# Chunk 0's diagonal by `v` and the identity in an attention-and-MLP kernel, with fewer idle products and late weights in halves

## The chip, the core and the metric

The kernel runs on one core of a Trainium2 chip. The metric is the device time of one execution in microseconds. In the texts the engines are called PE (TensorE, the matrix engine), DVE (VectorE), ACT (ScalarE), POOL (GpSimd) and SP (SyncE, which here only issues DMAs). "q" counts the four pairs of heads in a chunk of tokens.

## The reference

First a linear attention with a decay `w` and a bonus `u` for the present token, then a two-layer MLP with a leaky activation.

```python
B, H, S, D = 4, 8, 768, 48                       # r, k, v
for t in range(S):
    cur = np.einsum('bhd,bhe->bhde', u[None] * kt, vt)
    y[:, :, t] = np.einsum('bhd,bhde->bhe', rt, state + cur)
    state = w[None, :, :, None] * state + np.einsum('bhd,bhe->bhde', kt, vt)
...
x = y.transpose(0, 2, 1, 3).reshape(B * S, H * D)          # 3072 x 384
h = x @ w_in                                               # 384 x 2048
g = np.maximum(h, 0.0) + alpha * np.minimum(h, 0.0)
return (g @ w_out)                                         # 2048 x 384
```

## The kernel before

The 768 positions are cut into six chunks of 128. In chunk 0 (`first_chunk(q)`, once for each pair q of heads) the attention needs no state. DVE scales `r` and `k` by powers of the decay (L431) and multiplies them elementwise into `prod` (L500). PE sums `prod` with `u` (`c_sum`, L507), which gives the diagonal of the score matrix, `cu`: one number for each position, head and batch, in eight columns of a bank. PE makes the scores of all pairs of positions (`scores`, L442). ACT copies the sums (L511) and writes eight blocks "identity times `cu`" into two `base` tiles (L449); DVE copies the scores of earlier positions over them by a mask (`copy_predicated`, L453); PE multiplies `base` by `v` (`out`, L463). The output is split in a high and a low part, `xh` and `xl` (L389, L392 on ACT, L378, L379 for the last pair), of which pieces are moved to other partitions by small DMAs (`lower`, L367). PE also turns `k` (`turn`, L295), ACT copies it (`kk`, L299), PE makes the chunk's state (L489), and ACT copies that to `T` (L494).

Then come the hidden tiles: 16 tiles of 128 hidden units for each chunk. For one tile and one chunk `m_in` makes nine products of 512 columns (L678: high by high, high by low and low by high, for three slices of the input), ACT and DVE make the activation's high part `gh` and low part `gl` (L686 to L691), and `m_out` adds nine products (L712) into three banks. The order of the tiles is chunk 0 tiles 0 to 8, chunk 1 tiles 0 to 8, chunk 0 and then chunk 1 tiles 9 to 15, then the chunks 2 to 5. The attention of later chunks (`prepare` and `burst`, L533 to L650) is placed between them. The weights of a tile arrive as one load of 768 KB (`wraw`, L323, two buffers) and are put together in `weights`: ACT L343, DVE L345, L347, L350, ACT L353 (`wh`), DVE L354 (`wl`).

A function `warm` (L233) adds a bf16 product of the identity whose result nobody reads, an idle product. It writes the columns 128 to 511 of the bank that also holds chunk 0's diagonal sums. 23 of them stand at the program's start, and `with_warm(n, ...)` puts n ahead of a group of products.

The Python code does not set the engines' order itself. Each `add` hands a planner an engine, an estimated time, the tiles read and written, and a rank; `Plan.in_order` then chooses, for all engines together, what stands next. A new estimate or rank therefore moves other work too.

## Time and profile before

| | |
|---|---|
| median of three runs | 486.32 us (486.3 to 486.8) |
| profiled execution | 486.93 us |
| its span in the trace | 485.2 us |
| around the span | 1.73 us |
| PE busy | 476.6 us, 98% of the span, 4644 records |
| DVE busy | 310.8 us, 64% |
| ACT busy | 247.2 us, 51% |
| POOL busy | 43.5 us, 9% |
| granted clock of PE, mean | 0.995 |

The span begins with the first instruction that the profiler recorded and ends with the last; the execution's own time is a little longer. All starts in the rows below count from the span's start. A row's length runs to the end of the result, so rows of pipelined products overlap; what a group costs its engine is the distance from its start to the next group's.

### The profile page before, as it was taken

To read this page: it belongs to the slowest core of one execution; us is meant where nothing else is said; L and a number is where in the kernel's file an instruction comes from. 1 tells how busy PE (TensorE), PEld (TensorE's weight loads), DVE (VectorE), ACT (ScalarE), POOL (GpSimd) and SP (SyncE) were. 2 spreads that over 40 slices of the span, in tenths; PEclk is the share of its full clock that TensorE was granted. 3 is DMA by queue.
4 is the path that set the end of the run, shared out by engine and by line. 5 is a ranking of instruction groups with operands and counts; after the bars stand their busy time and mean duration, and the time that the engine had idled before them with its cause. 6 is when DMAs were issued, how large, how long until landed. Compare 5 with 4: busy or idle time off the path is not lost.

```text
span 485.2 us, 11237 instructions
## 1 busy us (share of the span) xinstructions
PE 476.6 (98%) x4644; PEld 387.5 (80%) x4644; DVE 310.8 (64%) x518; ACT 247.2 (51%) x578; POOL 43.5 (9%) x49
## 2 busy tenths in 40 slices
PE   8999999999999999999999999999999999999994
PEld 5778878888888888888888888888888878888883
DVE  7789999999786785855755655745644534333331
ACT  5889866776555552553553643444642333433222
POOL 2000010012211011101202202202000000000000
PEclk9999999999999999999999999999999999999998
DMA  8675776642243641431121341121210000100002
GB/s 238 193 209 187 225 242 190 228 157 66 72 131 106 187 136 57 136 103 36 58 83 37 118 119 37 54 75 33 95 26 1 1 1 0 67 0 0 1 1 70
DMA packets 23752, 45.82 MB, mean 94 GB/s; under 512 B 3856, under 2 KB 11408, under 8 KB 23696
## 3 DMA queue, kind: packets, MB, share of 16 engines
q1 hardware_dynamic: 23552, 44.92, 29.6%
q8 instruction: 38, 0.62, 0.6%
q14 instruction: 18, 0.15, 0.1%
q10 hardware_dynamic: 144, 0.13, 0.1%
HBM read 36.38 MB, written 6.29 MB: 88 GB/s over the span
## 4 chain that ended last, share of the span: by engine, by line
PE 88%; DVE 7%; ACT 2%; DMA 1%; issue 1%; POOL 0%; ACTq 0%; DVEq 0%; POOLq 0%
PE acc L712 40%; PE bank L678 38%; PE bank L612 2%; PE acc L233 2%; PE bank L622 2%; PE bank L591 2%; PE bank L584 1%; DVE wl L354 1%; DMA wraw<-wall 1%; DVE wx L350 1%; DVE wx L347 1%; DVE g L687 1%; DVE wx L345 1%; DVE gl L691 1%; ACT wx L343 1%
## 5 line engine op out<-in xcount | busy, mean ns | idle before, releaser
L687 DVE SCALAR_TENSOR_TENSOR g<-bank,alph,g 128x512 f32<-128x512 f32 x96 | 71.9, 748 | 107.0 <-ACT g L686 106.3
L686 ACT ACTIVATE g<-bank 128x512 f32<-128x512 f32 x96 | 57.3, 597 | 137.0 <-PE bank L678 136.5
L678 PE MATMUL bank<-xh,wh 128*128 128x512 f32 x288 | 113.0, 392 | 0.0
L678 PE MATMUL bank<-xh,wl 128*128 128x512 f32 x288 | 112.2, 390 | 0.1
L678 PE MATMUL bank<-xl,wh 128*128 128x512 f32 x288 | 112.1, 389 | 0.0
L691 DVE TENSOR_TENSOR gl<-g,gh 128x512 fp32r<-128x512 f32 x96 | 69.5, 724 | 41.6 <-ACT gh L690 41.4
L690 ACT ACTIVATE gh<-g 128x512 fp32r<-128x512 f32 x96 | 60.5, 630 | 66.1 <-DVE g L687 65.9
L712 PE MATMUL acc<-gh,wh 128*128 128x512 f32 x288 | 83.6, 396 | 0.0
L712 PE MATMUL acc<-gh,wl 128*128 128x512 f32 x288 | 82.0, 391 | 0.0
L712 PE MATMUL acc<-gl,wh 128*128 128x512 f32 x288 | 81.7, 390 | 0.0
L678 PEld LDWEIGHTS bank<-xh,wh 128*128 128x128 f32 x288 | 54.0, 188 | 11.6 <-ACT kk L299 0.3
L678 PEld LDWEIGHTS bank<-xh,wl 128*128 128x128 f32 x288 | 54.1, 188 | 11.5 <-DVE wl L354 0.5
L678 PEld LDWEIGHTS bank<-xl,wh 128*128 128x128 f32 x288 | 54.1, 188 | 11.3
L712 PEld LDWEIGHTS acc<-gl,wh 128*128 128x128 f32 x288 | 54.0, 188 | 11.3
L712 PEld LDWEIGHTS acc<-gh,wl 128*128 128x128 f32 x288 | 53.8, 188 | 11.4
L712 PEld LDWEIGHTS acc<-gh,wh 128*128 128x128 f32 x288 | 52.7, 188 | 11.2
L547 POOL TENSOR_TENSOR rr<-rr,kk 128x384 f32<-128x384 f32 x16 | 22.5, 1405 | 286.2 <-DMA kk<-vkr 227.1
L558 ACT ACTIVATE base<-ident,cu 128x64 f32<-128x64 f32 x160 | 41.5, 337 | 1.0 <-DVE cu L553 0.9
L379 DVE TENSOR_TENSOR xl<-bank,xh 48x256 fp32r<-48x256 f32 (+1 forms) x66 | 28.4, 430 | 1.5
L533 DVE TENSOR_TENSOR raw<-raw,W 112x512 f32<-112x512 f32 x40 | 26.7, 682 | 0.8 <-DMA raw<-rk 0.8
L378 ACT ACTIVATE xh<-bank 48x256 fp32r<-48x256 f32 (+1 forms) x66 | 25.5, 386 | 2.5 <-PE bank L622 1.0
L643 DVE COPY_PREDICATED base<-strict,bank 128x256 f32<-128x256 uint8 x40 | 17.3, 442 | 4.4 <-PE bank L591 4.4
(102 smaller groups left out, 388.2 us busy)
## 6 DMA issues: line engine op xcount, KB each, us to landing
wraw<-wall SPq DMA_DIRECT2D x16, 768.0 KB, 4.7
raw<-rk SPq DMA_DIRECT2D x46, 224.0 KB, 3.9
v<-vkr SPq DMA_DIRECT2D x24, 192.0 KB, 3.6
rr<-vkr SPq DMA_DIRECT2D x16, 192.0 KB, 2.5
kk<-vkr SPq DMA_DIRECT2D x16, 192.0 KB, 3.4
oT<-o SPq DMA_DIRECT2D x12, 256.0 KB, 2.2
oT<-g SPq DMA_DIRECT2D x5, 256.0 KB, 2.8
xh<-xh SPq DMA_DIRECT2D x36, 32.0 KB, 2.0
```

What stands on the lines that cost most here:

```text
L378: add("ACT", us, lambda: nc.scalar.activation(to(h), view(), AF.Copy), r=[src], w=refs(h), rank=rank)
L379: add("DVE", us + 0.1, lambda: nc.vector.tensor_tensor(out=to(l), in0=view(), in1=to(h), op=ALU.subtract), r=[src] + refs(h), w=refs(l), r ...
L533: add("DVE", 0.72, lambda t=t, tab=tab: nc.vector.tensor_tensor(out=t().rearrange("p b (j t) -> p (b j) t", t=span), in0=t().rearrange("p ...
L547: add("POOL", 1.2, lambda: nc.gpsimd.tensor_tensor(out=rt(), in0=rt(), in1=k(), op=ALU.mult), r=[k] + ([wh[12]] if c == 2 else []), w=[rt] ...
L558: add("ACT", 0.32, lambda g=g, b=b: nc.scalar.activation(base()[:, g, b], ident2(), AF.Copy, scale=cu()[:, g, b:b + 1]), r=[cu, ident2], w ...
L643: add("DVE", 0.42, lambda g=g: nc.vector.copy_predicated(base()[:, g], strict2()[:, None, :].broadcast_to([128, B, HI]), A[g]()[:, 0:256]. ...
L678: nc.tensor.matmul(hp()[:, :], a[i]()[:, k], x[c]()[:, k], start=(k == 0 and j == 0), stop=(k == NK - 1 and j == 2))
L686: add("ACT", 0.6, lambda: nc.scalar.activation(g(), hp()[:, :], AF.Copy), r=[hp], w=[g], rank=n - 100)
L687: add("DVE", 0.75, lambda: nc.vector.scalar_tensor_tensor(out=g(), in0=hp()[:, :], scalar=alph()[:, i:i + 1], in1=g(), op0=ALU.mult, op1=A ...
L690: add("ACT", 0.64, lambda: nc.scalar.activation(gh(), g(), AF.Copy), r=[g], w=[gh], rank=n - 100)
L691: add("DVE", 0.73, lambda: nc.vector.tensor_tensor(out=gl(), in0=g(), in1=gh(), op=ALU.subtract), r=[g, gh], w=[gl], rank=n - 99)
L712: nc.tensor.matmul(banks[k](), a[i]()[:, NK + k], x(), start=(begin and j == 0), stop=(end and j == 2))
```

## The change

For chunk 0 the diagonal no longer goes into the score matrix. DVE multiplies `v` by the sums into a tile `vc`, straight from the bank (L475 of the changed kernel), and `out` adds four products of `vc` with the identity for each pair (L495). The `base` tiles get zeros once (`zeroed`, L441) in place of the scaled identity, and the copies `cu` of chunk 0 are gone. Two POOL memsets clear the two tiles that `vc` uses (L375). The number of idle products falls, from two to one or from two or one to none, and the block at the start has five of 512 columns, one for each bank, and 16 of 384 in place of 23 of 384. Raw weights from tile 10 on come in two loads, and tile 2's load is put behind chunk 0's `lower` DMAs.

```diff
     def warm(into):
...
+        idle(into()[:, 128:512])
+
+    def idle(into):
+        x, n = ident().bitcast(mybir.dt.bfloat16), into.shape[1] // 2
+        nc.tensor.matmul(into.rearrange("p (a f) -> p a f", a=2), x[:, 0:128],
+                         x[:, None, 0:n].broadcast_to([128, 2, n]), start=True, stop=True, skip_group_check=True)
...
+        if i < NF - 6:
+            return load(t, lambda: nc.sync.dma_start(t().rearrange("p f a -> p (f a)"), wall[i].bitcast(U32)), 768, rank,
+                        behind)
+
+        for j in range(2):
+            load((t, j), lambda j=j: nc.sync.dma_start(
+                t()[:, DM * j:DM * (j + 1)].rearrange("p f a -> p (f a)"),
+                wall[i].bitcast(U32)[:, 2 * DM * j:2 * DM * (j + 1)]), 384, rank)
...
+            if i == 2:
+
+                for t, at in first_lower:
+                    p.after.update(o for o, part, wr in plan.log[t] if wr and part == at and o.eng == "SP")
...
+    spread = [sb([128, B, 2 * HI], "gh", 3, F32R, mv) for _ in range(2)]
+    for t in spread:
+        add("POOL", 0.6, lambda t=t: nc.gpsimd.memset(t().bitcast(F32), 0.0), w=[t], rank=-70)
...
+    def zeroed(n):
+        if n not in bases:
+            bases[n] = [sb([128, B, L], "gl", 3, F32, mv) if n else sb([128, B, L], "base", 3) for _ in range(2)]
+            for t in bases[n]:
+                add("ACT", 0.6, lambda t=t: nc.scalar.activation(
+                    t(), ident()[:, None, :].broadcast_to([128, B, L]), AF.Copy, scale=0.0), r=[ident], w=[t], rank=-93 + n)
+        return bases[n]
...
-        with_warm(2, 1.05, scores, r=[r, k0], w=A, rank=q - 90).after.add(first)
-        base = [sb([128, B, L], "gl", 3, F32, mv) if q % 2 else sb([128, B, L], "base", 3) for _ in range(2)]
-        for g in range(2):
-            for b in range(B):
-                add("ACT", 0.39, lambda g=g, b=b: nc.scalar.activation(
-                    base[g]()[:, b], ident(), AF.Copy, scale=cu()[:, g, b:b + 1]), r=[cu, ident], w=[(base[g], b)],
-                    rank=-60 + q)
+        with_warm(1, 1.05, scores, r=[r, k0], w=A, rank=q - 90).after.add(first)
+        base = zeroed(q % 2)
+        vc = spread[q % 2]
+        add("DVE", 0.55, lambda: nc.vector.tensor_tensor(
+            out=vc().bitcast(F32).rearrange("p b (g e) -> p g b e", g=2)[:, :, :, 0:D],
+            in0=v().rearrange("p (g b) e -> p g b e", g=2), op=ALU.mult,
+            in1=bank()[:, 8 * q:8 * q + 8].rearrange("p (b g) -> p g b", g=2)[:, :, :, None].broadcast_to([128, 2, B, D])),
+            r=[v, (bank, q)], w=[vc], rank=10 * q - 77)
...
-                        stop=b == B - 1, skip_group_check=True)
-
-        last_out[:] = [with_warm(2, 0.95, out, r=[v] + base, w=[y], rank=q - 85)]
+                        stop=False, skip_group_check=True)
+            for b in range(B):
+                nc.tensor.matmul(y()[0:112, b * L:(b + 1) * L], vc().bitcast(F32)[:, b, 0:112], ident(), start=False,
+                                 stop=b == B - 1, skip_group_check=True)
+
+        last_out[:] = [with_warm(0, 1.45, out, r=[v, vc, ident] + base, w=[y], rank=q - 85)]
...
-            with_warm(1, 0.5, lambda: turn(t, k0), r=[k0, ident], w=[t], rank=-84 + q)
+            with_warm(0, 0.5, lambda: turn(t, k0), r=[k0, ident], w=[t], rank=-84 + q)
...
-            with_warm(1, 0.75, product, r=[k, v], w=[U], rank=-45 + q)
+            with_warm(0, 0.75, product, r=[k, v], w=[U], rank=-45 + q)
...
-        first = with_warm(2 if mine != sums else 0, 0.56, c_sum, r=[prod, uw], w=[mine], rank=sum_rank)
...
+        first = with_warm(1 if mine != sums else 0, 0.56, c_sum, r=[prod, uw], w=[mine], rank=sum_rank)
...
-    add("PE", 6.7, lambda: [warm(bank) for _ in range(23)], r=[ident], w=[(bank, "warm")], rank=-1000)
+
+    add("PE", 6.7, lambda: [idle(t) for t in plan.banks] + [warm(bank) for _ in range(16)], r=[ident], w=[(bank, "warm")], rank=-1000)
```

How the planner's order moves is shown at three places. The first is PE at the diagonal sums and the scores of chunk 0's second pair; `acc_135` (before) and `acc_140` (after) are the bank with the sums and the idle products' results, and a bracket names the engine or DMA queue that a row waits for. Before:

```order
L233 MATMUL acc_135<-ident 128x384 [waits Activation_49]
L233 LDWEIGHTS ident
L233 MATMUL acc_135<-ident 128x384
L507 MATMUL acc_135<-uw,g 64x2 [waits DVE_49]
L507 MATMUL acc_135<-uw,g 64x2 x7
L233 LDWEIGHTS ident
L233 MATMUL acc_135<-ident 128x384
L233 LDWEIGHTS ident
L233 MATMUL acc_135<-ident 128x384
```

After:

```order
L236 MATMUL acc_140<-ident 128x384
L538 MATMUL acc_140<-uw,g 64x2 [waits DVE_49]
L538 MATMUL acc_140<-uw,g 64x2 x7
L236 LDWEIGHTS ident
L236 MATMUL acc_140<-ident 128x384 [waits DVE_49]
```

One idle product has left each pair, and the wait for ACT, which copied the sums out of the bank, has become a wait for DVE at the second idle product.

The second place is DVE from the scaling of the third pair's `k` on. Before (`base` and `gl` are the tiles that the mask writes, `g` is `prod`):

```order
L431 TENSOR_TENSOR raw<-raw,W_78 112x512 [waits DMAHW6_49]
L431 TENSOR_TENSOR o<-o,W_79 112x512 [waits DMAHW7_49]
L453 COPY_PREDICATED base<-strict,bank_117 128x512 [waits PE_49,Activation_49]
L500 TENSOR_TENSOR g<-raw 112x512 [waits DVE_49]
L453 COPY_PREDICATED base<-strict,bank_118 128x512 [waits PE_49,Activation_49]
```

After (`gh` is `vc`):

```order
L459 TENSOR_TENSOR raw<-raw,W_78 112x512 [waits DMAHW6_49]
L475 TENSOR_TENSOR gh<-v,acc_140 128x2x4x48 [waits DMAHW1_49,PE_49]
L481 COPY_PREDICATED base<-strict,bank_117 128x512 [waits Activation_49]
L481 COPY_PREDICATED base<-strict,bank_118 128x512 [waits Activation_49]
L531 TENSOR_TENSOR g<-raw 112x512 [waits DVE_49]
L475 TENSOR_TENSOR gh<-v,acc_140 128x2x4x48 [waits DMAHW2_49,PE_49]
```

The product `vc`, which waits for the load of `v`, now stands right behind the third pair's scaling and ahead of both masks of the first pair; the fourth pair's scalings have moved behind.

The third place is SP, the queue that issues the DMAs, around the end of chunk 0. Before:

```order
L367 DMA xh<-xh_394 16x512 x4
L323 DMA wraw<-wall 128x1536
L367 DMA xh<-xh_394 16x512
L404 DMA raw<-rk 112x512
L367 DMA xh<-xh_394 16x512
L367 DMA xl<-xl_469 16x512 x6
L406 DMA v<-vkr 128x384 x2
```

After:

```order
L383 DMA xh<-xh_318 16x512 x4
L421 DMA raw<-rk 112x512 x3
L383 DMA xh<-xh_318 16x512
L383 DMA xl<-xl_432 16x512 x4
L383 DMA xh<-xh_318 16x512
L383 DMA xl<-xl_432 16x512 x2
L423 DMA v<-vkr 128x384 x4
L577 DMA rr<-vkr 128x384
L327 DMA wraw<-wall 128x1536 x2
```

Tile 2's load `wraw` has moved from among the parts of `xh` to behind all parts, four loads of `v` and one of `rr`.

In the same way the second tile's low weights `wl` now stand on DVE ahead of the first steps of the third tile, chunk 1's sums of one pair stand on PE ahead of the second tile's products, and the third tile's nine products stand behind the next burst of chunk 1, with which also the first `m_out` products have moved ahead of it.

## Rows read from the trace of the kernel before

**Rows 1.** The waits of PE: what it waited for, total us, times, longest.

```profile
PE bank L507 <- DVE g L500: 0.4, 1, 0.4
```

**Rows 2.** PE's timeline: start, length (us), engine, line, operation, tiles, number of instructions.

```profile
1.48 6.58 PE L233 MATMUL acc<-ident 128*128 128x384 bf16 x25 [1.48 <-POOL ident L257]
7.99 0.63 PE L507 MATMUL acc<-uw,g 112*64 112x2 f32 x16
...
11.51 0.50 PE L233 MATMUL acc<-ident 128*128 128x384 bf16 x2
11.93 1.16 PE L442 MATMUL acc<-raw 48*128 48x128 f32 x16
...
21.94 1.09 PE L463 MATMUL bank<-base,v 128*64 128x128 f32 x16
22.96 0.34 PE L233 MATMUL acc<-ident 128*128 128x384 bf16 x1
23.13 0.55 PE L295 MATMUL bank<-ident,raw 112*128 112x112 f32 x4
...
29.38 0.34 PE L233 MATMUL acc<-ident 128*128 128x384 bf16 x1
29.64 0.67 PE L489 MATMUL bank<-v,kk 128*64 128x48 f32 x16
30.26 0.60 PE L295 MATMUL bank<-ident,raw 112*128 112x112 f32 x4
...
30.92 0.50 PE L678 MATMUL bank<-xh,wh 128*128 128x512 f32 x1
...
35.01 0.39 PE L678 MATMUL bank<-xh,wl 128*128 128x512 f32 x1
...
43.01 1.13 PE L612 MATMUL bank<-raw,T 48*48 48x64 f32 x32
...
45.84 0.60 PE L295 MATMUL bank<-ident,raw 112*128 112x112 f32 x4
```

**Rows 3.** Tile `v`, 4 to 14 us: its loads (duration ns), and their time to landing.

```profile
L406 SPq DMA_DIRECT2D v<-vkr x4: 327/378/430, 5.0 to 7.1; - x4
...
DMA to landing us min/median/max: 6.2/6.6/6.8
```

**Rows 4.** DVE's line L411 over the whole run: duration ns min/median/max, first and last start.

```profile
L411 DVE TENSOR_TENSOR kk<-kk,whalf x16: 541/546/1371, 101.8 to 332.5; 128x384 f32<-128x384 f32 x16
```

**Rows 5.** ACT's timeline, 24 to 27 us.

```profile
24.37 0.87 ACT L353 ACTIVATE wh<-wx 128x768 fp32r<-128x768 f32 x1
...
25.53 1.61 ACT L392 ACTIVATE xl<-bank 112x512 fp32r<-112x512 f32 x3
```

**Rows 6.** DVE by lines, 4 to 32 us (busy, mean ns, idle before).

```profile
L453 DVE COPY_PREDICATED gl<-strict,acc 128x512 f32<-128x512 uint8 x4 | 2.9, 737 | 0.6 <-ACT gl L449 0.6
L453 DVE COPY_PREDICATED base<-strict,bank 128x512 f32<-128x512 uint8 x4 | 2.9, 727 | 1.9 <-ACT base L449 1.9
...
L345 DVE TENSOR_SCALAR wx<-wx 128x768 uint32<-128x768 uint32 x3 | 1.7, 561 | 1.4 <-ACT wx L343 1.4
```

**Rows 7.** DVE's timeline: a scaling of chunk 0, and tile 1's last step.

```profile
9.82 0.68 DVE L431 TENSOR_TENSOR raw<-raw,W 112x512 f32<-112x512 f32 x1
...
33.60 0.95 DVE L354 TENSOR_TENSOR wl<-wx,wh 128x768 fp32r<-128x768 f32 x1
```

**Rows 8.** SP's timeline: the issues of DMAs.

```profile
26.56 3.78 SPq L367 DMA_DIRECT2D xl<-xl  x6
```

**Rows 9.** Tile `wraw`, 0 to 70 us: its loads' time to landing.

```profile
DMA to landing us min/median/max: 4.5/6.1/8.8
```

**Rows 10.** Windows around the end: us, busy of PE, PEld, DVE, ACT, POOL, granted clock, DMA.

```profile
470.00:478.70 8.70, 8.70 (x39) 6.91 (x37) 2.15 (x4) 3.06 (x5) 0.00 (x0) 1.00 0.06 24
478.70:480.70 2.00, 0.03 (x1) 0.00 (x0) 0.42 (x1) 0.38 (x1) 0.00 (x0) 1.00 0.74 258
480.70:485.00 4.30, 0.00 (x0) 0.00 (x0) 0.00 (x0) 0.00 (x0) 0.00 (x0) 0.50 0.09 28
```

More of the change, by code (lines that the diff above doesn't have):

```diff
@@ L231, in warm @@
     def warm(into):
-        x = ident().bitcast(mybir.dt.bfloat16)
-        nc.tensor.matmul(into()[:, 128:512].rearrange("p (a f) -> p a f", a=2), x[:, 0:128],
-                         x[:, None, 0:192].broadcast_to([128, 2, 192]), start=True, stop=True, skip_group_check=True)
+        idle(into()[:, 128:512])
[3 more added lines that the diff above has]
+                         x[:, None, 0:n].broadcast_to([128, 2, n]), start=True, stop=True, skip_group_check=True)
     def with_warm(n, us, fn, r, w, rank):
@@ L317, in half_table @@
             pt()[:, :].rearrange("p (m g e) -> p m g e", m=P, g=2)[:, :, :, 0:D], AF.Copy), r=[pt], w=[whalf], rank=-62)
-    raws = {}
+    raws, first_lower = {}, []
     def raw_weights(i, rank, behind=()):
         t = raws[i] = sb([128, 2 * DM, 2], "wraw", 2, U32)
-        p = load(t, lambda: nc.sync.dma_start(t().rearrange("p f a -> p (f a)"), wall[i].bitcast(U32)), 768, rank, behind)
-        return p
+        if i < NF - 6:
[5 more added lines that the diff above has]
+                wall[i].bitcast(U32)[:, 2 * DM * j:2 * DM * (j + 1)]), 384, rank)
     def weights(i, need):
         if i not in raws:
-            raw_weights(i, need - 9)
+            p = raw_weights(i, need - 9)
+            if i == 2:
+                for t, at in first_lower:
+                    p.after.update(o for o, part, wr in plan.log[t] if wr and part == at and o.eng == "SP")
         raw = raws[i]
@@ L367, in dma @@
                     nc.sync.dma_start(t()[to, k].bitcast(F32), y()[HI * g + 16 * k:HI * g + 16 * (k + 1)].bitcast(F32))
+                first_lower.append((t, (k, g)))
                 add("SP", 0.45, dma, r=[top[name]], w=[(t, (k, g))], rank=-40 if c == 0 else -8, kb=32)
@@ L415, in u_rows @@
         return t()[0:112, at:at + B * D].rearrange("p (b e) -> p b e", b=B)
+    bases = {}
+    def zeroed(n):
[5 more added lines that the diff above has]
+        return bases[n]
     def first_chunk(q):
@@ L433, in first_chunk @@
                 r=[W[q]], w=[t], rank=10 * q + j - 90)
-        cu = sb([128, 2, B], "cu", 2)
-        first = diagonal(q, r, k0, cu, bank, slice(8 * q, 8 * q + 8), (bank, q), 10 * q - 88, -95 + q, -70 + q)
+        first = diagonal(q, r, k0, None, bank, slice(8 * q, 8 * q + 8), (bank, q), 10 * q - 88, -95 + q, -70 + q)
         A = [psum() if q % 2 == 0 else pb([128, NT], f"acc{g}") for g in range(2)]
@@ L508, in c_sum @@
                                      stop=True, skip_group_check=True)
-        first = with_warm(2 if mine != sums else 0, 0.56, c_sum, r=[prod, uw], w=[mine], rank=sum_rank)
-        add("ACT", 0.2, lambda: nc.scalar.activation(
-            cu(), sums()[:, cols].rearrange("p (b g) -> p g b", g=2), AF.Copy), r=[mine], w=[cu], rank=copy_rank)
+        first = with_warm(1 if mine != sums else 0, 0.56, c_sum, r=[prod, uw], w=[mine], rank=sum_rank)
+        if cu:
+            add("ACT", 0.2, lambda: nc.scalar.activation(
+                cu(), sums()[:, cols].rearrange("p (b g) -> p g b", g=2), AF.Copy), r=[mine], w=[cu], rank=copy_rank)
         return first
```

## The prediction

> **What bounds the kernel now.** I read the waits of TensorE (PE) first, then its timeline, then the views of those engines that feed it. After its start PE waits at one place for .4 us and at another for less [rows 1]: from 1.48 on it has work without a gap, so the time is the sum of what stands in PE's queue. A saving has to shorten that queue, and it lasts only as long as the data come earlier too. The prelude of chunk 0 ends where the first hidden tile starts, at 30.92 [rows 2]; that place is the measure of most of this change. DVE is the engine with the least room behind it. While it prepared chunk 0 it lay idle .6 + 1.9 + 1.4 = 3.9 us, waiting for ACT's base tiles and for ACT's first step of the weights [rows 6].
>
> **The parts, one by one.** All times are of the profiled execution, 486.93 us (its span of 485.2 and 1.73 around it), which lies .6 above the median of 486.32; the sum is a difference, and I take it off the median.
>
> *Opening block.* 25 idle products take 1.48 to 7.99 [rows 2]. The new block has 22, with 9088 columns in place of 9600: 512 fewer, 1.3 products of 384 at the .17 that one takes later (22.96 to 23.13) [rows 2]: -.2 us.
>
> *The wait for `v`.* This is the one new wait on PE that I can price. DVE's new product `vc` reads pair 0's diagonal sums in the bank in which the idle products write, and the order shows that the second idle product of pair 1 waits for DVE. PE stood there at 11.51; without the block's .2 and two halves of a pair (.42 the pair, 11.51 to 11.93 [rows 2]) it comes at about 10.9. But `vc` needs pair 0's `v`. The first of the four `v` loads is issued at 5.0, and they take 6.2 to 6.8 us [rows 3]; so it lands between 11.2 and 11.8, and I take 11.8, since the loads of all four pairs stand ahead of it. `vc` itself does not occur before. Its nearest row is a product of the same 128x384 shape on DVE, median 546 ns [rows 4]; one operand now lies in a bank, and the bounds are .5 and the .74 of a DVE operation of 512 columns on a bank [rows 6]. It ends at 11.8 + .55 = 12.35, and PE goes on at 12.4: a wait of 1.5 us (bounds .8 and 1.7). Counted against before, PE is .9 late at this place.
>
> *Idle products behind that place.* Between 11.51 and the last turn before the hidden tiles, 30.26, PE spends 18.75 us [rows 2]. In it lie nine pairs at .42 = 3.8, four single products at .17 (as 22.96 to 23.13) and four at .26 (29.38 to 29.64) = 1.7 [rows 2], together 5.5. Five single ones stay, at half a pair, .21: 1.05. So -4.45. Whether the group ahead of a removed idle product also gets shorter no row shows cleanly; it can only add to the gain, and I leave it out.
>
> *Identity products.* Eight f32 products of 128 columns take 21.94 to 22.96, .1275 each [rows 2]. Sixteen more: +2.05 (bounds 1.7, at a seventh less when nothing follows of another kind, and 2.2).
>
> *Check's product*, a short one between the turn at 30.26 and 30.92 [rows 2], leaves the prelude and comes back later: about -.1 here, 0 in all.
>
> The start of the hidden tiles follows: 30.92 + .9 - 4.45 + 2.05 - .1 = 29.3, a gain of 1.6 us.
>
> *Does ACT keep up?* ACT loses 32 `base` activations and four copies and gets four zeroings early, of which each step takes about .5 (as three of 112x512 take 1.61 [rows 5]): 2.0 us while it waits for the tables and for PE's first sums; without that cover PE's turn of the half table would come that much later. The last turn before the tiles waits for ACT's `T`. PE gives pair 2's output at 12.4 + the 11.45 from 11.51 to 22.96 less 3.6 of idle products, + 1.5 for twelve identity products, + 1.05 = 22.8. From there ACT has `xh`, two pairs of `kk`, two `xl`, `wh` (.87), `xh`, `xl`, a pair of `kk`, `xh` and `T`; with a pair of `kk` and each of the others at the half us of an `xl` that is ten halves and .87 [rows 5], 5.9 us: 28.7. PE wants it at 30.26 - 1.6 = 28.7. So ACT is just in time and I set its cost at nothing; bounds 0 and .5.
>
> *Does DVE keep up?* The low part of tile 1's weights is made by 33.60 + .95 = 34.55, and PE first uses it at 35.01 [rows 2, 7]. In the new order PE wants it at 35.01 - 1.6 and, because the sums of one pair now stand ahead of tile 1, .6 later: 34.0. Ahead of it on DVE there is more: four `vc` (2.0) and one more scaling (.6); and less: two steps of tile 2's weights (.56 and .95 [rows 6, 7]) and four tiny operations of the check (.4), 1.9. Idle time falls from 3.9 to the 1.3 for `v` (the scaling that stands ahead of `vc` as it stood before ends at 9.82 + .68 = 10.5 [rows 7]) and something up to .7 while `vc` and the masks follow PE. The net is +2.6 - 1.9 - 3.9 + 2.0 = -1.2: ready at 33.4, in time by .6. Tile 2's products have moved behind a burst (43.01 to 45.84 [rows 2]) and behind 16 products of 512 columns (.223 each, 8.70 us for 39 [rows 10]), so its weights are wanted at about 43.
>
> *Weight loads.* Halves from tile 10 on: PE waits for no weights there before, and six more DMA issues of under .5 us lie on an idle queue; 0 in the sum, and without that cover still under .5 for one tile. Tile 2's load, now behind chunk 0's lower parts, is rival three. Two memsets on POOL lie on an engine with nothing else due then: 0.
>
> Sum: -1.6 us, nearly all of it in the first 30 us, and no part of the stretch from 70 us on changes. 486.93 - 1.6 = 485.3 for the profiled execution, **484.7** against the median. With the bounds (wait .8 to 1.7, identity 1.7 to 2.2, shorter neighbours up to .5, ACT up to .5) the case itself spans 483.9 to 485.5.
>
> **A rule to weigh against this.** At the end of the program the granted clock is still 1.00 for 2.0 us after the last product, and .50 after that [rows 10]; that is the upper of the two levels, 2.4 GHz, then the lower, 1.2. PE's new wait is 1.5 us, shorter than that, so by the row the clock stays and the sum holds. The Trainium skill, "TensorE: Matmul & The Clock Gate", section "HAM oscillation — how this bites in real kernels", says that pauses of PE between groups of products send the clock back to half and that the products after the pause then run cold; by it, with fewer idle products left, the wait would cost a second start at the low level.
>
> **Rival one: the clock falls after the wait for `v` (chance .20).** For: the idle products are what PE did when it had nothing else, and 23 of them go. Against: the wait is shorter than the 2.0 us above, and PE has real products on both sides. The price of a low start can be read off the opening block: 25 products take 6.5 us where 25 at .17 would take 4.25, so 2.3 [rows 2]. -1.6 + 2.3 = +.7: 487.0, and 486.0 if half of the price lies under waits that are there anyway: no change that can be told.
>
> **Rival two: DVE gives the gain back (chance .17).** The margin of .6 at tile 1 rests on DVE's idle time falling by 1.9. Once 1.3 us or more remain beside the wait for `v` (the new `vc` stands in one queue with the masks, and behind it wait the masks, PE's outputs and ACT's `xh`), each further us is a wait of PE at the first tiles. If the idle time stays as it was, DVE is 1.9 late, PE loses 1.3, and the gain is .3: 486.0, the range of this case 485.4 to 486.4.
>
> **Rival three, slower: tile 2's raw weights come late (chance .13).** Before, the load stood between the lower parts; the six `xl` parts end at 26.56 + 3.8 = 30.3 [rows 8]. Now it stands behind all of them, four `v` and one `rr`. The parts come about 2 us earlier, then five issues of about .5 (an issue alone is .33 to .43 [rows 3]): issued at 30.8. Loads of this tile land after 4.5 to 8.8 us, median 6.1 [rows 9]: 36.9, at worst 39.6. From the landing ACT needs .9 and DVE, in the new order, eight operations up to `wl`, four of tile 2's (.56 and three of .95), four others of some 2.5, less .08 of overlap each: 5.3. So 43.1 against the 43 at which PE wants it. Every us of landing later than 37 is a us of PE, and DVE's later tiles shift with it. At 39.6 the loss is 2.5, +.9 in all: 487.2; with one more us, 488.2. For: the margin is none at the median. Against: half of the loads shown land sooner, and this one has few others beside it.
>
> **How the numbers follow.** The forecast has .50: 484.7. The rivals have .20, .17 and .13. What a measurement of this kernel can tell from no change is about 0.2%, 1 us: below 485.35 is faster, above 487.29 slower. Faster: .50 and a little of rival two, .52. Slower: most of rival three and the end of rival one, .12. Same: .36. The range of 8 in 10 goes from the lower bound of the forecast's own case, 483.9, to the 487.2 at which rival three starts to show.
>
> **What would show it.** In the changed profile PE's idle product of pair 1 waits for DVE at about 11, for 1.5 us, and DVE idles there for the `v` load. The first hidden tile starts near 29.3. PE has no wait above .5 between there and 70, and the clock reads 1.00 from 7 to 478. If the hidden tiles start at 29.3 and the end comes as before, look for a wait of PE between 33 and 60 for `wl` (rivals two and three). If the products after 12.4 are spaced twice as far, it is rival one. The prediction is wrong if the wait for `v` is longer than 1.7 us or if PE waits for ACT in the prelude by more than .5.

## The result, and the profile after

The changed kernel takes 490.57 us (median of 16 runs, 487.33 to 492.99); the kernel before, run beside it, takes 486.81 (16 runs, 485.52 to 487.93). The ratio is 1.0075, interval 1.0058 to 1.0091: slower by 3.8 us, where a gain of 1.6 was forecast. The 16 times go with the mean granted clock of PE, which was measured for each execution: 487.33 us at .996, 492.99 at .987, and 14 of the 16 below .995, where the executions of before beside the experiments lie between .995 and .999. By an estimate from the medians of the clock (.991 against .998, over 490 us) some 3.4 of the 3.8 us are time lost at a low clock. The profiled execution took 492.12 us with a span of 490.4, 5.2 longer than before's. "Before" below is the kernel before, "after" the changed one, and "the start" is the first product of the first hidden tile, 30.92 us in before [rows 2].

After's waits of PE, in the form of [rows 1]:

```profile
PE bank L654 <- ACT seen_y L669: 1.8, 1, 1.8
PE bank L236 <- POOL ident L260: 1.5, 1, 1.5
PE bank L616 <- ACT kk L302: 0.8, 1, 0.8
PE acc L236 <- DVE gh L475: 0.7, 1, 0.7
PE bank L710 <- DVE wl L367: 0.5, 1, 0.5
PE bank L298 <- ACT T L525: 0.4, 1, 0.4
```

The 1.5 at the program's start is in before too [rows 2]. The others are 4.2 us where before had .6 (.4 [rows 1], and .2 for `xh` at 67). Their places stand in PE's timeline, in the form of [rows 2]:

```profile
8.23 0.63 PE L538 MATMUL acc<-uw,g 112*64 112x2 f32 x16
...
10.85 0.63 PE L538 MATMUL acc<-uw,g 112*64 112x2 f32 x16
12.19 0.32 PE L236 MATMUL acc<-ident 128*128 128x384 bf16 x1 [0.71 <-DVE gh L475]
12.44 1.16 PE L469 MATMUL acc<-raw 48*128 48x128 f32 x16
...
14.07 1.09 PE L491 MATMUL bank<-base,v 128*64 128x128 f32 x16
15.09 1.13 PE L495 MATMUL bank<-ident,gh 128*112 128x128 f32 x8
16.05 0.33 PE L236 MATMUL acc<-ident 128*128 128x384 bf16 x1
...
30.84 0.60 PE L298 MATMUL bank<-ident,raw 112*128 112x112 f32 x4 [0.38 <-ACT T L525]
31.21 0.47 PE L710 MATMUL bank<-xh,wh 128*128 128x512 f32 x1
...
34.74 0.63 PE L616 MATMUL bank<-v,kk 64*64 64x48 f32 x31 [0.82 <-ACT kk L302]
...
44.02 0.69 PE L654 MATMUL bank<-base,v 64*48 64x64 f32 x16 [1.79 <-ACT seen_y L669]
44.64 0.96 PE L538 MATMUL bank<-uw,g 112*64 112x2 f32 x16
45.53 1.65 PE L744 MATMUL acc<-gh,wl 128*128 128x512 f32 x3
...
48.68 1.48 PE L744 MATMUL acc<-gh,wh 128*128 128x512 f32 x3
```

Three things are to be seen. The start is at 31.21, not at 29.3. The four identity products of a pair (an f32 product shows as two records, so x8) take 15.09 to 16.05, .24 each, beside .13 for each of the eight ahead of them (14.07 to 15.09). And from 45 on three products of 512 columns take twice the usual time: 48.68 to 49.96, 1.28, where three at the .223 of [rows 10] take .67. The windows say why (columns as in [rows 10]):

```profile
13.00:15.00 2.00, 2.00 (x32) 1.65 (x28) 2.00 (x5) 0.55 (x2) 0.00 (x0) 1.00 1.03 320
...
45.00:46.00 1.00, 1.00 (x13) 0.98 (x12) 1.00 (x3) 0.97 (x2) 0.00 (x0) 0.50 0.03 10
...
50.00:51.00 1.00, 1.00 (x4) 0.81 (x3) 1.00 (x4) 0.87 (x2) 0.00 (x0) 0.50 0.91 151
...
52.00:53.00 1.00, 1.00 (x6) 0.81 (x5) 0.43 (x1) 0.00 (x0) 0.00 (x0) 1.00 0.97 401
```

The granted clock is at its upper level (2.4 GHz) after the wait of .71 for `vc`, and at its lower (1.2 GHz) for 6 us after the wait of 1.79. What was late there is a load. SP's timeline, then ACT's:

```profile
34.54 0.86 SPq L327 DMA_DIRECT2D wraw<-wall  x2
```

```profile
41.93 0.89 ACT L356 ACTIVATE wx<-wraw 128x768 f32<-128x768 f32 x1 [2.37 <-DMA wraw<-wall]
42.73 0.54 ACT L302 ACTIVATE kk<-bank 128x192 f32<-128x192 f32 x2
43.15 0.63 ACT L722 ACTIVATE gh<-g 128x512 fp32r<-128x512 f32 x1
43.80 0.17 ACT L669 ACTIVATE seen_y<-bank 1x2 f32<-1x2 f32 x1
```

Tile 2's raw weights are issued at 34.54, behind all parts of chunk 0, and land 7.4 us later. ACT stands 2.37 us in its queue for them, and behind that step waits `seen_y`, which PE needs.

The price of the low clock is read against a run that passes the same place at the upper level, `e5_own_bank` (below):

```profile
43.88 0.96 PE L744 MATMUL acc<-gh,wl 128*128 128x512 f32 x3
...
47.25 0.39 PE L710 MATMUL bank<-xh,wh 128*128 128x512 f32 x1
```

The account of this execution against before: the start +.3; later waits of 1.8, .8 and .5 where before had .4 and .2, +2.5; the low clock +2.8 (45.53 to 51.24 is 5.7 for what takes 3.4 in e5, with .3 more in the `c_sum` ahead and .2 in the product behind). That is 5.6 against the 5.2 of the spans. The products of tiles 2 to 4 stand in another order in the two kernels, and I leave the .4 open.

### The profile page after: what moved, and what is told of

It is laid out like the page before. It is cut to its first block, busy times and chain, and to the rows that moved or that the text cites. A ratio compares the mean times of both kernels' runs of the same rounds, so it can differ in the third digit from the quotient of the medians.

```text
span 490.4 us, 11223 instructions
## 1 busy us (share of the span) xinstructions
PE 478.5 (98%) x4650; PEld 391.7 (80%) x4650; DVE 312.0 (64%) x522; ACT 239.2 (49%) x546; POOL 45.2 (9%) x51
## 4 chain that ended last, share of the span: by engine, by line
PE 89%; DMA 4%; DVE 3%; ACT 2%; SPq 1%; issue 0%; ACTq 0%; DVEq 0%
PE acc L744 40%; PE bank L710 38%; DMA wraw<-wall 3%; PE bank L644 2%; PE bank L654 2%; PE bank L623 2%; PE bank L616 1%; DMA v<-vkr 1%; PE bank L495 1%; PE bank L491 1%; SPq L421 1%; DVE wx L363 1%; ACT wx L356 1%; PE acc L469 0%; DVE wl L367 0%
## 5 line engine op out<-in xcount | busy, mean ns | idle before, releaser
L744 PE MATMUL acc<-gh,wl 128*128 128x512 f32 x288 | 83.4, 396 | 0.0
L654 PE MATMUL bank<-base,v 64*48 64x64 f32 x640 | 19.1, 216 | 1.8 <-ACT seen_y L669 1.8
```

The source lines that it names most:

```text
L654: nc.tensor.matmul(where(g, b, j), v0()[s, g * B + b], base0()[s, g, b], start=False, stop=(crossed == 1 and e == 0), skip_group_check=True)
L744: nc.tensor.matmul(banks[k](), a[i]()[:, NK + k], x(), start=(begin and j == 0), stop=(end and j == 2))
```

## The experiments

All were timed in five rounds, each beside before on its own chip. Medians of runs taken at different times stand beside different runs of before, so the ratio is the surer figure. Each run gives its median, its ratio to before with the 95% interval, and what its own profiled execution shows.

**What an identity product costs.** `e3_ident_halves`, after with every identity product as two of half the width:

```diff
-                nc.tensor.matmul(y()[0:112, b * L:(b + 1) * L], vc().bitcast(F32)[:, b, 0:112], ident(), start=False,
-                                 stop=b == B - 1, skip_group_check=True)
+                for rows in (slice(0, HI), slice(HI, 112)):
+                    nc.tensor.matmul(y()[rows, b * L:(b + 1) * L], vc().bitcast(F32)[:, b, rows], ident(), start=False,
+                                     stop=b == B - 1, skip_group_check=True)
```

> The changed kernel with each identity product split into two, of 64 and of 48 of the 112 columns of vc, which go to the two column halves of PE as out's own products do; 32 products in place of 16, all else in the same order. Theory B (a product over the full width costs .24, and two over half the width each run side by side): the four products of a pair take .96 us in the changed kernel and about .5 here, so the prelude gets 1.9 us shorter up to the wait for ACT's T, and the hidden tiles start at 29.5 to 30.3 in place of 31.2. The end follows only in part, since tile 2's load stays late: 488.5 to 490.5. Rival (the price is by the number of products): the group takes 1.9 us, the hidden tiles start near 35, 492 to 495.

489.26 us, 1.0080 (1.0051 to 1.0109). PE's timeline at the second pair's output, where the clock is at its upper level again:

```profile
20.71 1.04 PE L496 MATMUL bank<-ident,gh 128*48 128x128 f32 x16
21.69 0.34 PE L236 MATMUL acc<-ident 128*128 128x384 bf16 x1
```

Eight halves take .98, as four whole ones took .96: .12 for a half, .24 for a whole. The price goes with the width, and the prediction's .1275 was that of a half.

`e5_own_bank` is told below. On it rest `e9_no_ident`, without the identity products:

```diff
-            for b in range(B):
-                nc.tensor.matmul(y()[0:112, b * L:(b + 1) * L], vc().bitcast(F32)[:, b, 0:112], ident(), start=False,
-                                 stop=b == B - 1, skip_group_check=True)
```

> e5 (the idle product ahead of the scores in its own bank) without the sixteen identity products, so that chunk 0's outputs lack the diagonal's share; DVE still makes vc. It measures what the identity products cost. In the profiles four of them take .96 us, 3.8 in all. If all of it lies on PE's path, the hidden tiles start at 26.7 in place of 30.5 and PE's wait for T grows by nothing. If ACT or DVE then set the pace of the prelude, the start moves by less than 3.8 and the difference shows as waits of PE for masks, T or wl: start 27.5 to 29.5, time 485 to 487. If tile 2's load and chunk 1's v loads stay where they are, the end moves less than the start.

and `e10_turned`, in which PE writes `vc` turned (a transposition against the identity) and adds `out`'s products onto it:

```diff
+                nc.tensor.matmul(y()[0:112, b * L:(b + 1) * L], vc().bitcast(F32)[:, b, 0:112], ident(), start=b == 0,
+                                 stop=False, is_transpose=True, skip_group_check=True)
```

> e5 with vc turned by PE's transposition in place of the f32 product with the identity, written first, with the products of out added onto it. Four turns of k take .31 to .39 us in both profiles, where four identity products take .96, so the prelude gets .6 shorter for each pair, 2.4 in all: the hidden tiles start at 28.1 by that sum, later by what PE then waits for masks (DVE's vc and masks come at the same times as in e5) and for T. 485.5 to 487.5.

`e9_no_ident`: 487.17 us, 1.0027 (1.0004 to 1.0049), its start at 28.24. `e10_turned`: 485.74 us, 1.0002 (.9989 to 1.0014), its start at 28.23; e5 starts at 30.52. PE's timeline of `e10_turned`:

```profile
16.42 0.65 PE L489 MATMUL bank<-ident,gh 128*112 128x128 f32 x4
17.00 1.09 PE L494 MATMUL bank<-gl,v 128*64 128x128 f32 x16
```

Four transpositions take .58, .145 each, in one record each. In their profiles both start 2.3 us earlier than e5. In e9 that is 2.3 of the 3.8 us of identity products; the rest went mostly into waits for `kk`, `xl` and `T`. In e10 the transpositions save 1.5 of product time; they also stand ahead of `out`'s products now, where PE in e5 stands for the masks, and .2 lies in the opening block. In the times `e10_turned` shows it (2.1 below e5 by the medians, 1.1 by the ratios, the intervals just overlapping). `e9_no_ident` does not: its runs spread from 484.31 to 490.65, at mean clocks from .998 down to .990.

**The wait for `v`.** In after, the idle product ahead of pair 1's scores writes the bank from which DVE reads the sums for `vc`, and so waits for `vc`, and `vc` for `v`. `e5_own_bank` lets it write the scores' own bank, which takes the cause of the wait away:

```diff
-        p = add("PE", us + WARM * n, lambda: [warm(bank) for _ in range(n)] + [fn()], r=r + [ident] * (n > 0),
+        p = add("PE", us + WARM * n, lambda: [warm(into or bank) for _ in range(n)] + [fn()], r=r + [ident] * (n > 0),
...
-        with_warm(1, 1.05, scores, r=[r, k0], w=A, rank=q - 90).after.add(first)
+        with_warm(1, 1.05, scores, r=[r, k0], w=A, rank=q - 90, into=A[0]).after.add(first)
```

> The changed kernel in which the idle product ahead of a pair's scores writes into that pair's own score bank, not into the bank with the diagonal sums; the order is the same, but PE no longer waits there for DVE's vc. Four of the five profiles of the changed kernel and of e1 to e4 show the granted clock at .50 for 3 to 7 us right after that wait (.66 to 1.6 us long), and the fifth, the changed kernel's own, shows it after the wait at 44. Theory D (the wait for vc and the low clock behind it are the larger loss): PE has no wait above .5 near 11.5, the clock reads 1.00 from 7 to 25, the hidden tiles start at 30.5 to 31, and the median falls by 1.5 to 3, to 487.5 to 489; the late load of tile 2 is left. Rival (the clock falls because idle products are few): it falls in the prelude here too, and the time stays at 490 to 491.

487.88 us, 1.0025 (1.0005 to 1.0045): 2.7 less than after's median (2.4 by the ratios), the intervals apart, from one edit that removes no work. PE's waits:

```profile
PE bank L616 <- DMA v<-vkr: 1.0, 1, 1.0
PE bank L654 <- ACT seen_y L669: 0.9, 1, 0.9
PE acc L538 <- DVE g L531: 0.7, 1, 0.7
```

```profile
10.26 0.63 PE L538 MATMUL acc<-uw,g 112*64 112x2 f32 x16
...
14.40 1.13 PE L495 MATMUL bank<-ident,gh 128*112 128x128 f32 x8
```

```profile
7.00:30.00 23.00, 21.94 (x318) 18.07 (x318) 20.08 (x33) 9.82 (x22) 0.00 (x0) 1.00 0.75 212
```

The wait for `vc` is gone, the clock is 1.00 from 7 to 478 in this execution, the start is at 30.52, and the late waits remain. The wait itself was cheap: from pair 1's sums to pair 0's identity products after takes 4.24 us with it (10.85 to 15.09) and e5 takes 4.14 without it (10.26 to 14.40), since PE then stands for the masks `base`. The .6 by which e5 is ahead at 10.26 lies in the opening block. What e5 saves is clock: five of its 12 executions, at mean clocks of .996 to .998, take 485.54 to 487.81 us, and seven, at .992 to .994, 487.68 to 489.57. In those seven the clock was low for longer, at a place that no trace shows.

`e8_diag_only` has the diagonal's part alone: before with the change's lines on `spread`, `zeroed`, `vc` and L495, all of before's idle products and its loads. Against the change's lines it differs in these, among others:

```diff
-        with_warm(1, 1.05, scores, r=[r, k0], w=A, rank=q - 90).after.add(first)
+        with_warm(2, 1.05, scores, r=[r, k0], w=A, rank=q - 90).after.add(first)
...
+        last_out[:] = [with_warm(2, 1.45, out, r=[v, vc, ident] + base, w=[y], rank=q - 85)]
```

> The kernel before with the diagonal by vc and the identity alone; idle products, opening block and loads as before. Each identity product costs .24 us in the changed kernel's profile, so sixteen add 3.8 to the prelude, and the wait for vc adds about .5; nothing is taken out of PE's queue. By that sum the hidden tiles start near 35 and the time is 489 to 491. If the idle products are cover for other engines rather than length, the end moves less: 487 to 488. The clock should stay at 1.00, since the idle products are all there.

`e16_diag_own` is the same with e5's edit.

> e8 (the diagonal alone, all idle products of the kernel before kept) with the idle products ahead of the scores in the scores' own bank. e8's profile has a wait of 1.05 us for vc and then the clock at .50 from 12.3 to 19.8 us, 3.7 us lost, with all idle products there. If the wait is what lowers the clock, both go: the clock reads 1.00 from 7 to 25, and the median falls from 497.1 by 3 to 5, to 492 to 494. If the mix of products lowers it, 496 to 498.

`e8_diag_only`: 497.09 us, 1.0194 (1.0165 to 1.0223). `e16_diag_own`: 494.10 us, 1.0172 (1.0151 to 1.0192). Windows of e8, then of e16:

```profile
13.00:14.00 1.00, 1.00 (x10) 1.00 (x12) 1.00 (x2) 0.00 (x0) 0.00 (x0) 0.50 1.08 313
```

```profile
13.00:14.00 1.00, 0.88 (x13) 0.63 (x14) 1.00 (x3) 0.00 (x0) 0.00 (x0) 1.00 1.13 387
```

With the wait (1.05 us) the clock is .50 right behind it, though no idle product is missing; without it the clock stays. The medians differ by 3.0, but the intervals overlap. The mean clocks part the runs: e8's two executions at .997 and .998 take 494.89 and 493.43 us, within e16's 493.41 to 496.20, and its four at .993 and below take 496.67 to 499.82.

Both are above the 489 to 491 that was expected of e8. e16 starts at 37.71, 6.8 later than before. Beside the 3.8 of the identity products its profile has 39 idle products between the opening and the start where before has 30 (the planner adds some where it foresees a gap), and PE stands 2.05 us at 71 for nothing that the profile shows. In e8's profile it stands 2.67 at 76, and the clock is .50 again from 77 to 80.

`e6_fill_v` is after with eight more idle products, in the scores' bank, ahead of the one that waits.

> The changed kernel with eight more idle products (1.3 us at the upper level) ahead of pair 1's scores, writing into their own bank, which need not wait for vc; the waiting idle product is still behind them. PE is busy in the place of its wait. If the pause is what lowers the clock: 1.00 from 7 to 25, the wait below .5, the hidden tiles start near 31.2 as in the changed kernel's profile, median 487.5 to 489. If the clock falls all the same, 490 to 492.

489.94 us, 1.0063 (1.0041 to 1.0085). A wait of .72 was left and the clock stayed up behind it, but it was .50 from 45 to 49, after a wait of 1.2 for `seen_y`. The interval overlaps after's: inconclusive.

**The idle products by themselves.** `e7_idles_only` is before with the new block and the new counts of idle products, nothing else.

```diff
-        with_warm(2, 1.05, scores, r=[r, k0], w=A, rank=q - 90).after.add(first)
+        with_warm(1, 1.05, scores, r=[r, k0], w=A, rank=q - 90).after.add(first)
...
-        last_out[:] = [with_warm(2, 0.95, out, r=[v] + base, w=[y], rank=q - 85)]
+        last_out[:] = [with_warm(0, 0.95, out, r=[v] + base, w=[y], rank=q - 85)]
```

> The kernel before with the new numbers of idle products alone (new opening block, 7 in place of 30 later); no product of vc, no identity products, loads as before. The planner orders anew. If PE's queue is all that counts, the hidden tiles start up to 4.4 us earlier than 30.92 and the time falls by up to 4. If ACT's base activations set the pace of the prelude (DVE waited 3.9 us for ACT there [rows 6]), PE gets waits on DVE's masks and ACT in place of idle products, some of them long enough for the clock to fall: 485 to 489.

489.76 us, 1.0072 (1.0054 to 1.0089), the clock never down after the opening. PE's waits:

```profile
PE bank L587 <- DMA v<-vkr: 2.2, 1, 2.2
...
PE bank L298 <- DVE xl L382: 1.4, 1, 1.4
PE bank L625 <- ACT seen_y L640: 1.3, 1, 1.3
```

4.5 us of products left the queue, and the kernel is 3 us slower: PE comes earlier to its data and stands for them. The planner also puts some loads elsewhere when PE's pieces are shorter: tile 2's is issued at 30.89, in before at 24.14. So this run doesn't separate the two. Beside the diagonal's part it is the other way round: e16, with before's idle products and loads, takes 494.10, and e5, with the changed kernel's, 487.88.

**Tile 2's load.** `e1_load_early` issues it right behind the step that frees its buffer, with the rest of the order kept; `e4_early_halves` is that and e3's halves.

```diff
+    order.remove(moved[0])
+    order.insert(order.index(freed[0]) + 1, moved[0])
```

> The changed kernel with one DMA issue moved: tile 2's raw weights are issued right behind the last read of their buffer (tile 0's third DVE step), as early as the buffer allows, and not behind all lower parts, v and rr; every engine's other work stands in the same order. Theory A (the late load is the cause): in the changed kernel it is issued at 34.5 and lands at 41.9, ACT stands at tile 2's first step from 39.6 to 41.9 with the burst's seen_y copy behind it, PE waits 1.8 us at 44.0, and then the granted clock is .50 from about 44.8 to 51.4, which costs 3.3. Issued near 26.6 it lands near 33; PE's wait at the burst falls below .3, the clock reads 1.00 from 7 to 478, and the median falls by about 5 us, to 485 to 486. Rival (the clock falls because idle products are gone, whatever the load does): the wait goes, a stretch at .50 stays, 488 to 489. Rival (identity products and DVE's new work are the loss): no change, 490 to 491.

> Both edits: tile 2's load early and the identity products in halves. By theories A and B together the losses of 5 and up to 1.9 us are gone: 483.5 to 485, and hidden tiles from 29.5 to 30.3. If ACT and DVE give the prelude's gain back, as e1: 485 to 486. If DVE is then late with tile 1's or 2's low weights, PE's waits for wl show it.

`e1_load_early`: 490.97 us, 1.0101 (1.0070 to 1.0132). `e4_early_halves`: 489.12 us, 1.0067 (1.0043 to 1.0092). The wait for `seen_y` is gone from both. In e1 PE waits 1.4 for a part of `xh` instead, and its start is at 33.96; in e4 it waits 1.6 for `wh`, start at 34.33. In both the clock is .50 for some 3 us behind the wait for `v`.

`e2_fill_wait` puts ten idle products under the wait for `seen_y`.

> The changed kernel with ten more idle products of 384 columns (about 1.6 us at the upper level) ahead of the second part of chunk 1's first full burst, where PE waits 1.8 us for ACT; nothing else moves. If the clock falls because PE pauses there, PE is busy through the pause, the clock reads 1.00 from 7 to 478, tile 2's load is as late as in the changed kernel and the burst's second part starts as late (near 44), but the 13 products behind it take 2.9 us and not 6: about 3.3 us less, 487 to 487.5. If the low stretch has another cause (fewer idle products in the prelude, or the mix of short products): the clock falls again, 490 to 491.

491.10 us, 1.0093 (1.0067 to 1.0118). That wait is .2 now, but the clock was down behind the wait for `v` (1.6), and again from 50 on, after 1.3 us in which PE stood and the profile shows nothing it waited for. Inconclusive on what it was made for.

`e17_not_behind_parts` is after without the rule that puts the load behind the parts, planned anew:

```diff
-            if i == 2:
-
-                for t, at in first_lower:
-                    p.after.update(o for o, part, wr in plan.log[t] if wr and part == at and o.eng == "SP")
```

> The changed kernel without the line that puts tile 2's load behind the lower parts, ordered anew by the planner: the load stands behind the parts all the same, but ahead of chunk 1's four v loads and rr, and tile 2's first step on ACT stands two places earlier. The wait for vc and the identity products are unchanged. If that line is what makes the change slow: 486 to 488. If the prelude's wait, clock and identity products are (e5, e9, e10), and the place of the load only moves waits (e11 to e15): 489.5 to 491.5.

489.03 us, 1.0063 (1.0046 to 1.0080): 1.5 less than after by the medians, .6 by the ratios, and the intervals overlap. Its waits of PE and its windows:

```profile
PE acc L236 <- DMA v<-vkr: 1.5, 1, 1.5
PE bank L298 <- ACT T L521: 0.4, 1, 0.4
PE bank L534 <- DVE g L527: 0.3, 1, 0.3
```

```profile
13.00:14.00 1.00, 1.00 (x12) 1.00 (x12) 1.00 (x3) 0.00 (x0) 0.00 (x0) 0.50 1.08 336
...
17.00:18.00 1.00, 1.00 (x8) 0.81 (x5) 0.04 (x1) 0.00 (x0) 0.00 (x0) 0.50 0.99 239
```

All late waits are .4 or less. But the load is issued at 33.90, only .6 earlier than in after, and PE comes 2.9 later to the start, at 34.12, so the late start alone gives the load time. What is lost here stands ahead of the start: the wait for `v`, and the half clock behind it. From there to the end of the span it is as fast as before (+3.2 at the start, +2.9 at the end).

`e13_behind` leaves the load and moves the first steps of tile 2 on ACT and DVE behind `seen_y` and tile 1's `gl`, and tile 3's first step behind the next `xh`.

```diff
+    for i, *ps0 in ((2, seens[0], lows[1]), (3, highs[0])):
+        at = max(order.index(p) for p in ps0)
+        late = [p for p in order[:at] if p in steps[i]]
+        order = [p for p in order[:at + 1] if p not in late] + late + order[at + 1:]
```

> The changed kernel with tile 2's first three steps on ACT and DVE moved behind the burst's seen_y copy and tile 1's gl, and tile 3's first step behind the xh of chunk 1's first pair; loads and PE's order as in the changed kernel. If ACT's queue, held by the late load, is what made PE wait 1.8 us at 44.0, seen_y comes at about 41 and PE has no wait for it; tile 2's wl still comes at 48, so up to 1 us may be waited for there. The wait for vc in the prelude is untouched, and so are the falls of the clock behind it: median 0.5 to 1.5 below the changed kernel's 490.6. If the load's landing itself is what is waited for, the wait only moves to wl: no change.

490.96 us, 1.0095 (1.0076 to 1.0115). Its waits of PE:

```profile
PE bank L714 <- DVE wl L368: 1.5, 2, 1.1
...
PE acc L236 <- DMA v<-vkr: 1.1, 1, 1.1
```

`seen_y` is in time and the weights themselves are late: the landing binds, whatever queues behind it.

The same moves on e5 and e10 stand apart from the wait for `v`. The load behind chunk 1's second `v`: `e11_own_mid`, `e12_turned_mid`; e13's edit: `e14_own_behind`, `e15_turned_behind`.

> e5 with tile 2's raw load moved forward in SP's queue by two v loads and one rr load: behind the second v of chunk 1 and no longer behind all four and rr. If the late landing of this load (ACT stands at tile 2's first step, and the burst's seen_y copy behind it) is worth the .9 us that PE waits there in e5, plus .5 for wl, the median falls by about 1 us to 486.5 to 487.2. If the loads only change places (the later v loads are then waited for), nothing: 487.5 to 488.5.

> e10 and e11 together. By the sums 484.5 to 486.5, at or below the kernel before (486.5). If the loads bind from 30 us on, as e11's second case, no better than e10.

> e5 and e13 together: neither the wait for vc nor the wait for seen_y. By the sums of e5's profile (487.9 with .9 us of seen_y) 486.5 to 487.5; within the spread of e5 if the landing is what binds.

> e10 and e13 together: vc turned by transposition, own banks, and ACT and DVE not held by tile 2's load. e10's profile starts the hidden tiles 2.7 us earlier than the kernel before and then waits 1.2 us for seen_y; without that 484.3 to 485.3 against 485.7 of e10 and 486.1 to 486.7 of the kernel before, so faster than both. If the landing binds, PE waits for wl at about 44 in its place: 485.5 to 486.

| kernel | median us | ratio (interval) | waits of PE in its profile |
|---|---|---|---|
| `e11_own_mid` | 487.01 | 1.0032 (1.0012 to 1.0052) | 1.8 for nothing shown, `base` .7, `wl` .4 |
| `e12_turned_mid` | 486.14 | 1.0005 (.9990 to 1.0020) | 1.2 for nothing shown, `xh` 1.2 |
| `e14_own_behind` | 487.78 | 1.0029 (1.0017 to 1.0042) | `wl` 1.2, `base` 1.0, `v` 1.0 |
| `e15_turned_behind` | 485.80 | .9988 (.9979 to .9997) | `wl` 1.8 |

The intervals overlap those of their bases (e5 1.0005 to 1.0045, e10 .9989 to 1.0014): moved by hand, the load gives one wait for another. In e11 the clock is .50 from 45 to 49 behind its 1.8; in the other three profiles it stays at 1.00.

**The best of it.** `e18_turned_free` is `e10_turned` without the rule on the load, planned anew.

> e10 (vc turned by transposition, idle products in the scores' own banks) without that line. If an earlier load lets the prelude's 2.7 us through to the end: 483.5 to 485. If chunk 1's v loads, now behind it, are waited for instead: 485 to 486.5, as e10, e12 and e15.

485.31 us (12 runs, 484.64 to 486.05), .9980 (.9971 to .9989): faster than both kernels. The load is issued at 28.63, in e10 at 30.88, with nearly the same start (28.39 and 28.23), and e10's wait of 1.2 for `seen_y` is gone. Its waits of PE and three windows:

```profile
PE bank L403 <- ACT xh L402: 0.7, 1, 0.7
PE bank L534 <- DVE g L527: 0.4, 1, 0.4
PE bank L298 <- ACT T L521: 0.4, 1, 0.4
```

```profile
7.00:30.00 23.00, 22.27 (x314) 17.38 (x312) 21.27 (x35) 11.72 (x27) 0.00 (x0) 1.00 0.74 215
30.00:60.00 30.00, 29.59 (x505) 24.15 (x507) 29.27 (x53) 24.95 (x65) 0.00 (x0) 1.00 0.67 219
60.00:478.00 418.00, 416.78 (x3806) 343.16 (x3800) 255.49 (x423) 196.74 (x441) 38.31 (x32) 1.00 0.25 78
```

The clock is 1.00 in all three, the start is at 28.39, 2.5 ahead of before, and 1.9 of it is still there at the end of the span. None of its 12 executions has a mean clock below .996.

## Why the prediction was wrong

**The term of the identity products was mis-sized.** The prediction put "+2.05" on sixteen, from a row whose products are of half the width (128*64). It took the number of columns that pass (128) as the whole of a product's size; the runs show that the width of the standing operand counts as well. At .24 they cost 3.8, beyond the upper bound of 2.2 as well. From PE's going on after the wait to the start the forecast had 12.4 to 29.3, 16.9 us; after took 12.19 to 31.21, 19.0. Of the 2.1 between them this term is 1.75 and ACT's late `T` .38; the clock stayed up in that execution and has no part in it.

**"By the row the clock stays" failed.** The wait was where the prediction had it, for the reason it gave, and PE went on at 12.2 where 12.4 was forecast; `vc` took .56 for .55. It lasted .7 for 1.5, since PE came later than thought: in this execution the opening block was no shorter (the first sums start at 8.23, in before at 7.99; 7.17 in e18's and 8.38 in e13's, with the same block), and a single idle product costs .25 (12.19 to 12.44) where .21 was put. But with it in the program, not filled, the granted clock was .50 for about 3 to 7 us behind it in seven of eight profiled executions (e1, e2, e3, e4, e8, e13, e17, after waits of .66 to 1.6 us; not in after's own). In the nine without it (e5, e9 to e12, e14 to e16, e18) the clock is 1.00 from 7 to 30. The row at the end of the program shows one fall, after a pause of 2.0 us; it doesn't show that a shorter one is safe. The Trainium skill, "TensorE: Matmul & The Clock Gate", section "HAM oscillation — how this bites in real kernels", says that pauses of PE for data between groups of products send the clock back. These seven agree in kind; the pauses of its example are longer than any wait here, so the falls behind .66 us and more go beyond what it states. Rival one, which the prediction gave .20, is true of most of the profiled executions that have the wait. The wait and what follows it cost 2.7 by e5's median against after's, 2.4 by the ratios (3.0 by e16's median against e8's, where the intervals overlap), and nearly all of it is the clock.

**Rival three came true as well.** The prediction called the margin of tile 2's load "none at the median". The load was issued at 34.5 where 30.8 was forecast: the parts ended at 30.9 where 28.3 was reckoned, and the five issues behind them took 3.5 for 2.5. It landed at 41.9 where 36.9 was forecast. The order of what suffers was partly wrong: not `wl` first, but `seen_y`, which stands in ACT's queue behind the step that waits for the load; with `seen_y` moved ahead, `wl` is late (e13). Without the rule on the load the late waits are gone (e17, where the late start helps; e18, where it does not); what that is worth in time the intervals leave between nothing and some 2 us.

**The idle products: a gain here, a loss by themselves.** "-4.45" was right as a count of what left the queue, and after's prelude has it: it is in the 16.9 us above, and the 2.1 that came on top have other names. But the prediction asked only of ACT and DVE whether the data come earlier. e7 shows that alone the removal is a loss of 3.0, in waits for `v`, `xl` and `seen_y`; how much of that is the later load of tile 2 is not shown.

**What held.** ACT is late for the last turn ahead of the start by .4 in after (forecast 0 to .5). DVE did not give the gain back at tile 1: PE's only wait for `wl` is .5, at 74, behind another load that took 7.3 us to land. From 75 us on after has no wait of PE, as forecast for the loads in halves, which were not tried apart. Removed one after the other, the three costs are 2.7 by the medians and 2.4 by the ratios (the wait for `v`, e5), 2.1 and 1.1 (identity products to transpositions, e10), .4 and 1.1 (the rule on the load, e18). Only the first step's intervals are apart; from after to e18 they lie far apart.

**What stays open.** What decides whether the clock falls. The length of a wait alone does not: after's own execution kept its clock behind .71 us while e1's lost it behind .66, and waits of 2.20 us (for `v`, e7), 2.05 (e16) and 1.59 (for `wh`, e4) passed with the clock at 1.00. Where e5's slower executions lost theirs is open too; of them the mean clock is known and no trace.

## What to carry to other kernels

Take the price of a product from a row with the same use of the array, its width and depth, and not with the same number of passing columns alone. When a new consumer reads a buffer in which filler work writes, the filler inherits its wait: give it a buffer of its own first, then measure the change. Filler on an engine that seems to be the bound may be covering a wait for data: taken out alone it lost 3.0 us here (e7), and with the rest of the change its time was won in the prelude. When the runs of one kernel spread, set their times beside the mean clock that is listed for each.

## What the runs showed of the hardware

An f32 product that takes the whole width costs .24, and one that takes 64 of its columns (L491) or 48 of its rows (L469: eight from 12.44 to 13.54) .13 to .14, as if two such ran side by side. An f32 transposition against the identity costs .145 and can be added onto by products that follow in the same bank.

The granted clock went from 2.4 to 1.2 GHz behind waits of .66 to 2.7 us with products on both sides, and was at the lower level for some 3 to 7 us. Other waits of up to 2.2 us left it at 2.4 GHz.

In five executions (e2, e8, e11, e12, e16) PE stood 1.2 to 2.7 us at one product while the profile shows nothing that it waited for. One such row, of e11's timeline:

```profile
44.09 0.50 PE L746 MATMUL acc<-gh,wl 128*128 128x512 f32 x1 [1.77 <-issue]
```

Its cause was not found.
